# Routing the tokens once for groups of blocks instead of once for each block

## The chip, the cores and the metric

The kernel runs on one core of a Trainium2 chip. The metric is the device time of one execution in microseconds (us). TensorE (PE) does the matrix products, VectorE (DVE), ScalarE (ACT) and GpSimd (POOL) the element work, SyncE (SP) issues most of the transfers. PEld is TensorE's loading of weights.

## The reference

Three layers follow one another on 8 batches of 576 tokens, 4608 tokens of 512 values. First a landmark attention with 8 heads of 64, for each batch:

```
q_lm, k_lm = means of 18 consecutive rows of q and of k           # 32 landmarks
A, Bm, C   = softmax(q k_lm'), softmax(q_lm k_lm'), softmax(q_lm k)
Z          = Bm' / (norms of Bm);  6 times: Z = 2 Z - Z Bm Z
x          = A Z C v
```

Then a mixture of 8 experts with one expert for each token, where the routing is computed from the attention's output, and at last a dense layer with a squared relu:

```
logits = x @ w_gate;  expert = argmax(logits)
gate   = exp(logits - max) / (sum + 1e-9), at the argmax           # = 1 / (sum + 1e-9)
y      = gate * (relu(x @ w1[expert]) @ w2[expert])
out    = relu(y @ w_in)^2 @ w_out
```

## The kernel before, in words

There are three stages: the attention (`phase_a`), the experts (`phase_m1`), the dense layer (`phase_m2`). The attention works on a block at a time; a block is one batch, and its 576 tokens lie as 96 partitions (`PR`) of 6 tokens each (`R`). A block passes through parts, each written as a generator whose steps end at a `yield`: `load*`, `front` (transposes of q and k, landmarks), `head` (the small matrix Bm), `mid` (C v), `newton` (the six iterations), `amap` (the map A), `xout` (logits, and the output rows sent to `x_rows` in HBM) and `rout` (the routing). Block 0's routing also turns the order of the experts (`ro["perm"]`, `ro["key"]`), from which `wpre` loads the first expert's weights ahead.

`xout` makes the logits on TensorE and DVE transposes them to `lg`, 96 partitions x 6 tokens x 32, of which 8 are used (line 592). `rout` (lines 612 to 687) takes from them, for each of a block's 6 columns of 96 tokens: the maximum, the one-hot choice `oh`, the sum of the exponentials, the gate `gt`, and the rank of each token among those of its expert. The rank counts the tokens of the same expert in earlier partitions (a triangle of ones), in earlier columns of the block (a matmul with ones for each column), and in the earlier blocks, whose counts are kept in `ro["cnt"]`; all of it is summed in one bank `pr` on TensorE (lines 652 to 656). The rank is split into a place within a tile of 128 tokens and the tile's base (`ro["a128"]`), and `ro["ohv"]` keeps for each column a matrix of the places, 96 x 128 (line 684, once for each column). A block's gate is sent to the last column of `x_rows` by a transfer of SP's queue (line 667). Line numbers are those of the kernel before.

Who reads the routing: `prer` runs once, behind the routing of block 5; from `oh`, `a128` and `ohv` of blocks 0 to 5 it makes the lists of tokens of the first three tiles (`gpre`, `spre`), and POOL gathers these rows from `x_rows` (line 84). `prea`, `preb` and `prec` work on those tiles (the experts' first products) while the last blocks' attention runs. `tiles` runs behind the routing of block 7 and makes the lists of all 46 tiles, and then the stage of the experts begins.

The order of the work is given by the table `WHEN`: for each part, and for some blocks of their own, the due times of its first and last step, in units of a block's period. The steps of all parts and blocks are sorted by due time and traced in that order; a part is traced only when those that it needs have been (`rout` needs `xout` of its block and the routing before it). The framework then lays out the queue of each engine from this order by estimated costs, and puts in the waits. Each engine works its queue in order. Of the tiles of the routing there are two buffers each (pool `as`).

Of the kernel before, what the change touches and what calls it, by code (L numbers as in the profile page):

```python
# [7 lines left out]
F32 = mybir.dt.float32  # L8
F16 = mybir.dt.float16
I32 = mybir.dt.int32  # L10
U32 = mybir.dt.uint32
AF = mybir.ActivationFunctionType
ALU = mybir.AluOpType
# [4 lines left out]
B, H, S, D = 8, 8, 576, 64  # L18
NE, DM, FF = 8, 512, 1024
DF = 2048  # L20
NT = B * S
PR, R = 96, 6
LM = 32
XW = DM + 1
# [6 lines left out]
NBIG = 6  # L31
GB = 3
NG = -(-B // GB)
LMS = (0, 0)
RHE = ("VPPA", "PPPP")
EVE, EVA, QP = 2, 0, 1
# [207 lines left out]
def phase_a(tc, cst, q, k, v, wg, x_rows, x2, ro, rt, w12, wb, held):  # L244
    nc = tc.nc
    V, P, ACT, PE = nc.vector, nc.gpsimd, nc.scalar, nc.tensor
    with (
# [12 lines left out]
        for i in range(2):  # L260
            t = a1.tile([128, 2, 4, 64], F32, name=f"bd{i}")
# [14 lines left out]
        def small():  # L276

            turns[0] ^= 192
            return nb[:, turns[0]:turns[0] + 192]
# [6 lines left out]
        def big(name):  # L286
            return psb.tile([128, 512], F32, tag="b", name=name)

        st = [dict() for _ in range(B)]

        def load(nm, src):
            def one(b):
# [10 lines left out]
        for i in range(2):  # L303
            t = a1.tile([128, 2, 256], F32, name=f"wbd{i}")
            P.memset(t, 0.0)
            wbds.append(t)
            t = a1.tile([128, 32], F32, name=f"nrm{i}")
            P.memset(t, 0.0)
            nrm.append(t)
            t = a1.tile([128, 2, 32], F32, name=f"G{i}")  # L310
# [3 lines left out]
        def front(b):  # L314
# [5 lines left out]
            for ti, nm in enumerate(("q", "k")):  # L320
# [3 lines left out]
                for hf in range(2):  # L324
# [10 lines left out]
                    yield  # L335
                m = 4 if LMS[ti] == 2 else 5
                for g in range(-(-24 // m)):
                    n = min(m, 24 - m * g)
                    pt = big("pt")
                    for i in range(n):  # L340
                        j, r = divmod(m * g + i, R)
                        PE.transpose(pt[:, PR * i:PR * i + PR], rhs[j // 2][:, r, 128 * (j % 2):128 * (j % 2) + 128],
                                     ident[:PR, :PR])
                    if LMS[ti] == 2 and g % 3 == 2:

# [235 lines left out]
        def xout(b):  # L581
            s = st[b]
            AT, wbd, G = s["AT"], s["wbd"], s["G"]

            pl = small()
            for qd in range(2):
                av = AT[:, qd].rearrange("p (r a) -> p r a", r=R)
                for g in range(3):
                    PE.matmul(pl[32 * g:32 * g + 32, 0:192], G[:, qd, :], av[:, :, 32 * g:32 * g + 32],
                              start=(qd == 0), stop=(qd == 1))  # L590
            s["lg"] = lg = asm.tile([PR, R, 32], F32, tag="lg", name="lg")
            V.transpose(lg.rearrange("p r e -> p (r e)"), pl[:PR, 0:192])
            yield
            rows = x_rows[b * S:(b + 1) * S, :].rearrange("(p r) c -> p r c", r=R)
            t0 = 0
            for n in (128, 128, 128, 96, 96):
                px = big("px")
                for qd in range(2):
                    PE.matmul(px[:n, 256 * qd:256 * qd + 256], AT[:, qd, t0:t0 + n], wbd[:, qd, :],
                              start=True, stop=True)  # L600
                xr = a1.tile([128, DM], F32, tag="xr", name="xr", bufs=3)
                ACT.activation(xr[:n], px[:n], AF.Copy)
                i = 0
                while i < n:
                    r, p0 = divmod(t0 + i, PR)
                    m = min(n - i, PR - p0)
                    nc.sync.dma_start(out=rows[p0:p0 + m, r, 0:DM], in_=xr[i:i + m])
                    i += m
                t0 += n
                yield  # L610

        def rout(b):

            s = st[b]
            lg = s["lg"][:, :, 0:NE]
            bc = slice(b * R, (b + 1) * R)

            def over(t):
                return t.rearrange("p (r o) -> p r o", o=1).to_broadcast([PR, R, NE])
            mx = asm.tile([PR, R], F32, tag="mxl", name="mxl")  # L620
            V.tensor_reduce(out=mx, in_=lg, axis=AX.X, op=ALU.max)
            yield
            eq = asm.tile([PR, R, NE], F32, tag="eq", name="eq")
            V.tensor_tensor(eq, lg, over(mx), op=ALU.is_equal)
            V.tensor_tensor(lg, lg, over(mx), op=ALU.subtract)
            yield

            V.tensor_tensor(eq, eq, ro["ev"].rearrange("p (o e) -> p o e", o=1).to_broadcast([PR, R, NE]), op=ALU.mult)
            ACT.activation(lg, lg, AF.Exp)
            yield  # L630
            m = asm.tile([PR, R], F32, tag="m", name="m")
            V.tensor_reduce(out=m, in_=eq, axis=AX.X, op=ALU.max)
            yield
            key = ro["key"]
            if b == 0:

                pm = small()
                PE.matmul(pm[:, 0:1], sel, m[:, 0:1], start=True, stop=True)
                V.tensor_scalar(ro["m0"], pm[:, 0:1], -1.0, None, op0=ALU.mult)
                V.tensor_scalar(ro["perm"], ro["e8"], ro["m0"][:, 0:1], None, op0=ALU.add)  # L640
                V.tensor_scalar(ro["perm"], ro["perm"], 7, None, op0=ALU.bitwise_and)
                V.tensor_scalar(key, ro["perm"], -1.0, 8.0, op0=ALU.mult, op1=ALU.add)
            oh = ro["oh"][:, bc]
            V.tensor_tensor(oh, key[:PR].rearrange("p (o e) -> p o e", o=1).to_broadcast([PR, R, NE]), over(m),
                            op=ALU.is_equal)
            se = asm.tile([PR, R], F32, tag="se", name="se")
            V.tensor_reduce(out=se, in_=lg, axis=AX.X, op=ALU.add)
            yield

            pr = big("pr")  # L650
            prv = pr[:PR, 0:R * NE].rearrange("p (r e) -> p r e", e=NE)
            PE.matmul(prv, ro["tri"], oh, start=True, stop=False)
            for r in range(R - 1):
                PE.matmul(prv[:, r + 1:], ro["ones"][:, 0:PR],
                          oh[:, r:r + 1].to_broadcast([PR, R - 1 - r, NE]), start=False, stop=False)
            PE.matmul(prv, ro["ones"][:, 0:PR],
                      ro["cnt"].rearrange("p (o e) -> p o e", o=1).to_broadcast([PR, R, NE]), start=False, stop=True)
            cr = asm.tile([PR, NE], F32, tag="cr", name="cr")
            V.tensor_reduce(out=cr, in_=oh.rearrange("p r e -> p e r"), axis=AX.X, op=ALU.add)
            V.tensor_scalar(se, se, 1e-9, None, op0=ALU.add)  # L660
            yield
            rk8 = asm.tile([PR, R, NE], F32, tag="rk8", name="rk8")
            V.tensor_tensor(rk8, prv, oh, op=ALU.mult)
            V.tensor_tensor(ro["cnt"], ro["cnt"], cr, op=ALU.add)
            gt = asm.tile([PR, R], F32, tag="gt", name="gt")
            V.reciprocal(gt, se)
            nc.sync.dma_start(out=x_rows[b * S:(b + 1) * S, DM:XW].rearrange("(p r) c -> p (r c)", r=R), in_=gt)
            yield
            rk = asm.tile([PR, R], F32, tag="rk", name="rk")
            V.tensor_reduce(out=rk, in_=rk8, axis=AX.X, op=ALU.add)  # L670
            yield
            ri = asm.tile([PR, R], I32, tag="ri", name="ri")
            V.tensor_copy(ri, rk)
            yield
            V.tensor_scalar(ri, ri, 127, None, op0=ALU.bitwise_and)
            yield
            bf = asm.tile([PR, R], F32, tag="bf", name="bf")
            V.tensor_copy(bf, ri)
            yield
            V.tensor_tensor(ro["a128"][:, bc], rk, bf, op=ALU.subtract)  # L680

            for r in range(R):
                c = b * R + r
                V.tensor_scalar(ro["ohv"][:, c], ro["ib"], bf[:, r:r + 1], ro["tv"][:, c:c + 1],
                                op0=ALU.is_equal, op1=ALU.mult)
                if r == 2:
                    yield
            yield

# [101 lines left out]
        def tiles(b):  # L791
# [39 lines left out]
            for h in range(NH):  # L831
# [13 lines left out]
                yield  # L845
            mk = T2([128, NG, NTL])
            piv = pi[:, 0:NG * NTL].rearrange("p (g t) -> p g t", g=NG)
            V.scalar_tensor_tensor(mk, piv, 0.0, ro["gof"], op0=ALU.is_gt, op1=ALU.mult)
# [103 lines left out]
        ev = []  # L952
# [9 lines left out]
def consts_r(nc, pool):  # L962
# [6 lines left out]
    def iota(t, pattern, base=0, mult=0):  # L969
# [633 lines left out]
```

## Time and profile before

| what | value |
| --- | --- |
| runs | 1357.51, 1361.43 and 1367.07 us, median 1361.43 |
| profiled execution | 1361.7 us |
| its span | 1360.0 us |
| its mean granted clock of TensorE | 0.985 of full speed |
| instructions | 41279 |
| PE busy | 1307.0 us, 96% of the span |
| DVE busy | 999.0 us, 73% |
| ACT busy | 737.3 us, 54% |
| POOL busy | 570.3 us, 42% |

The profile is of one execution. The busy time of an engine is the time in which it worked on some instruction; matmuls are pipelined and their ends are modelled, so a busy PE need not be PE at its peak. The attention stage is the first 283 us or so of the span, the experts run until about 680 us, the dense layer to the end.

### The profile page before, as it was taken

How to read it: one execution, taken by the hardware profiler on the slowest of the kernel's cores; microseconds unless marked ns; L12 is line 12 of the kernel's file. 1: busy time of each engine (PE TensorE's matmuls, PEld its weight loads, DVE VectorE, ACT ScalarE, POOL GpSimd, SP SyncE). 2: the span in 40 equal slices, each digit the busy share in tenths (PEclk: the TensorE clock that was granted, in tenths of full speed). 3: DMA queues.
4: the chain of work that ended last, by engine and by line, in shares of the span. 5: the costliest groups of instructions: out<-in, count | busy, mean ns of one | idle time of the engine just before them, and what ended most of it. 6: DMA issues, size and time to landing. Idle time of an engine off the chain costs nothing. (4 is left out here: it accounts for less than half of the span.)

```text
span 1360.0 us, 41279 instructions
## 1 busy us (share of the span) xinstructions
PE 1307.0 (96%) x16614; PEld 1074.3 (79%) x16614; DVE 999.0 (73%) x2655; ACT 737.3 (54%) x1388; POOL 570.3 (42%) x584
## 2 busy tenths in 40 slices
PE   6889889899999999999999999999999999999997
PEld 4556556567777777777688999999999999999996
DVE  6788998866768668875399767777777777767665
ACT  4445556444657456754356555555555555555554
POOL 4435554223434335564300344444444444454443
PEclk9788999999999999999999999999999999999999
DMA  9676965355577648465110111111111110111100
GB/s 209 134 183 155 208 154 136 95 198 137 172 197 239 144 116 238 122 147 105 59 32 25 24 33 33 33 21 29 33 33 33 33 31 19 33 33 33 33 2 32
DMA packets 131535, 126.68 MB, mean 93 GB/s; under 512 B 88704, under 2 KB 107136, under 8 KB 131328
## 3 DMA queue, kind: packets, MB, share of 16 engines
q1 hardware_dynamic: 121568, 93.92, 29.9%
q0 software_dynamic: 9120, 29.95, 6.8%
q8 instruction: 133, 2.18, 0.7%
q14 instruction: 74, 0.61, 0.2%
q10 hardware_dynamic: 640, 0.02, 0.0%
HBM read 215.03 MB, written 28.89 MB: 179 GB/s over the span
## 5 line engine op out<-in xcount | busy, mean ns | idle before, releaser
L1415 POOL TENSOR_TENSOR hq<-q,hq 128x896 f16<-128x896 f32 x127 | 239.8, 1888 | 308.4 <-ACT hq L1410 235.1
L1423 PE MATMUL o<-wo,hq 128*128 128x256 f16 x3024 | 355.7, 273 | 1.2 <-DVE hq L1415 0.7
L1423 PEld LDWEIGHTS <-hq 128*128 128x128 f16 x3024 | 290.0, 98 | 35.8 <-DVE hq L1415 1.0
L1389 DVE TENSOR_TENSOR q<-h,q 128x256 f32<-128x256 f32 x508 | 186.7, 388 | 135.4 <-ACT q L1398 110.2
L1403 ACT ACTIVATE q<-q 128x512 f32<-128x512 f32 x127 | 80.1, 630 | 220.1 <-DVE q L1389 220.1
L139 PE MATMUL py<-wb,hT 128*128 128x512 f16 x864 | 192.4, 379 | 0.1
L124 PE MATMUL ph<-xT,wb 128*128 128x128 f16 x1120 | 189.5, 219 | 1.9 <-ACTq L1042 1.9
L126 PE MATMUL ph<-xT,wb 128*128 128x128 f16 x1120 | 189.4, 219 | 0.5 <-DVEq L1042 0.5
L125 PE MATMUL ph<-xT,wb 128*128 128x128 f16 x1120 | 189.5, 219 | 0.0
L139 PEld LDWEIGHTS <-hT 128*128 128x128 f16 x864 | 83.0, 98 | 94.0 <-issue 0.4
L1410 ACT ACTIVATE hq<-q 128x896 f16<-128x896 f32 x144 | 136.0, 944 | 27.1 <-DVE q L1343 25.6
L1383 PE MATMUL h<-sx,wb 128*128 128x128 f16 x762 | 134.3, 219 | 0.8 <-DVE q L1389 0.8
L1384 PE MATMUL h<-sx,wb 128*128 128x128 f16 x762 | 134.3, 219 | 0.0
L1385 PE MATMUL h<-sx,wb 128*128 128x128 f16 x762 | 134.3, 219 | 0.0
L124 PEld LDWEIGHTS <-wb 128*128 128x128 f16 x1216 | 118.9, 98 | 6.3 <-ACTq L1042 2.2
L125 PEld LDWEIGHTS <-wb 128*128 128x128 f16 x1216 | 118.9, 98 | 4.6 <-issue 0.5
L126 PEld LDWEIGHTS <-wb 128*128 128x128 f16 x1216 | 118.9, 98 | 0.6 <-DVEq L1042 0.6
L130 DVE SCALAR_TENSOR_TENSOR hT<-ph,hT 128x512 f16<-128x512 f32 x72 | 49.6, 689 | 86.2 <-ACT hT L129 63.8
L129 ACT ACTIVATE hT<-ph 128x512 f16<-128x512 f32 x72 | 42.9, 595 | 123.5 <-PE ph L126 120.8
L1384 PEld LDWEIGHTS <-wb 128*128 128x128 f16 x1016 | 99.4, 98 | 0.9 <-issue 0.9
L1385 PEld LDWEIGHTS <-wb 128*128 128x128 f16 x1016 | 99.4, 98 | 0.0
L1383 PEld LDWEIGHTS <-wb 128*128 128x128 f16 x1016 | 99.3, 98 | 0.0
(349 smaller groups left out, 3169.2 us busy)
## 6 DMA issues: line engine op xcount, KB each, us to landing
stg<-in_moe_w SPq DMA_DIRECT2D x74, 2048.0 KB
qn<-in_q SPq DMA_DIRECT2D x16, 576.0 KB
kn<-in_k SPq DMA_DIRECT2D x16, 576.0 KB
vn<-in_v SPq DMA_DIRECT2D x16, 576.0 KB
fw<-in_moe_w_in SPq DMA_DIRECT2D x16, 512.0 KB
fw<-in_moe_w_out SPq DMA_DIRECT2D x16, 512.0 KB
x_rows<-xr SPq DMA_DIRECT2D x32, 192.0 KB
stg<-in_moe_w SPq DMA_DIRECT2D x16, 256.0 KB
```

The source lines that it names most:

```text
L124: nc.tensor.matmul(ph[:, f4], wh[:, c, fs], xT[:, c], start=(c == 0), stop=False)
L125: nc.tensor.matmul(ph[:, f4], wh[:, c, fs], xT[:, 4 + c], start=False, stop=False)
L126: nc.tensor.matmul(ph[:, f4], wl[:, c, fs], xT[:, c], start=False, stop=(c == 3))
L139: self.nc.tensor.matmul(py, hT[:, a, f], w[:, f], start=(i == 0), stop=(i == len(ps) - 1))
L1383: PE.matmul(ph[:, k], w(0, c), x(0, c), start=(c == 0), stop=False)
L1384: PE.matmul(ph[:, k], w(0, c), x(1, c), start=False, stop=False)
L1385: PE.matmul(ph[:, k], w(1, c), x(0, c), start=False, stop=(c == 1))
L1389: V.tensor_tensor(to, x, y, op=ALU.add)
L1403: ACT.activation(q[:, 3:7], q[:, 3:7], AF.Relu, scale=2.0 ** -8)
L1410: ACT.activation(hq[:, 0], s["q"], AF.Copy)
L1415: e.tensor_tensor(hq[:, 1], q, hq[:, 0], op=ALU.subtract)
L1423: PE.matmul(sums[k][:, z], hq[:, u, a], wo[:, x, f, w], start=(f == 0 and i == 0 and z == 0), stop=(f == 7 and i == 2), skip_group_check=True)
```

## The change

The routing is done for a group of blocks at a time, by the table `RG`: block 0; 1 and 2; 3, 4 and 5; 6; 7. The logits of a group's blocks are laid side by side in one tile `lg`. `rout` of a block that is not the last of its group returns at once; that of the last block runs the same instructions as before over `U` columns, 6 for each block of the group, in place of 6. The sums over earlier columns go over all columns of the group (line 654), so that the count of the earlier blocks is added once for each group. `ohv` is still made by one instruction for each column, and the gates are still sent by one transfer for each block, now one behind another. The due times in `WHEN` are unchanged.

```diff
+RG = ((0,), (1, 2), (3, 4, 5), (6,), (7,))
...
+        lgs, RM = {}, R * max(map(len, RG))
...
-            s["lg"] = lg = asm.tile([PR, R, 32], F32, tag="lg", name="lg")
+            grp = next(g for g in RG if b in g)
+            if b == grp[0]:
+                lgs[b] = asm.tile([PR, RM, 32], F32, tag="lg", name="lg")
+            o = R * (b - grp[0])
+            lg = lgs[grp[0]][:, o:o + R]
             V.transpose(lg.rearrange("p r e -> p (r e)"), pl[:PR, 0:192])
...
         def rout(b):
-            s = st[b]
-            lg = s["lg"][:, :, 0:NE]
-            bc = slice(b * R, (b + 1) * R)
+            grp = next(g for g in RG if b in g)
+            if b != grp[-1]:
+                return
+            b0, U = grp[0], R * len(grp)
+            lg = lgs[b0][:, 0:U, 0:NE]
+            bc = slice(b0 * R, b0 * R + U)
+
+            def wide(tag, last=(), dt=F32):
+                return asm.tile([PR, RM, *last], dt, tag=tag, name=tag)[:, 0:U]
...
-            mx = asm.tile([PR, R], F32, tag="mxl", name="mxl")
+            mx = wide("mxl")
             V.tensor_reduce(out=mx, in_=lg, axis=AX.X, op=ALU.max)
...
-            for r in range(R - 1):
+            for r in range(U - 1):
                 PE.matmul(prv[:, r + 1:], ro["ones"][:, 0:PR],
-                          oh[:, r:r + 1].to_broadcast([PR, R - 1 - r, NE]), start=False, stop=False)
+                          oh[:, r:r + 1].to_broadcast([PR, U - 1 - r, NE]), start=False, stop=False)
...
-            nc.sync.dma_start(out=x_rows[b * S:(b + 1) * S, DM:XW].rearrange("(p r) c -> p (r c)", r=R), in_=gt)
+            for i, c in enumerate(grp):
+                nc.sync.dma_start(out=x_rows[c * S:(c + 1) * S, DM:XW].rearrange("(p r) c -> p (r c)", r=R),
+                                  in_=gt[:, R * i:R * i + R])
...
-            for r in range(R):
-                c = b * R + r
+            for r in range(U):
+                c = b0 * R + r
                 V.tensor_scalar(ro["ohv"][:, c], ro["ib"], bf[:, r:r + 1], ro["tv"][:, c:c + 1],
                                 op0=ALU.is_equal, op1=ALU.mult)
-                if r == 2:
+                if r % 6 == 2:
                     yield
```

The other tiles of the routing (`eq`, `m`, `se`, `rk8`, `gt`, `rk`, `ri`, `bf`) are widened as `mx` is.

## Rows read from the trace of the kernel before

**Rows 1.** The page's part 1: busy us, share of the span, instructions.

```profile
PE 1307.0 (96%) x16614; PEld 1074.3 (79%) x16614; DVE 999.0 (73%) x2655; ACT 737.3 (54%) x1388; POOL 570.3 (42%) x584
```

**Rows 2.** Busy time by stretches of the span; the first line names the columns.

```profile
core 0: us, PE busy (x) PEld busy (x) DVE busy (x) ACT busy (x) POOL busy (x), PEclk, DMA share, GB/s
60.00:130.00 70.00, 65.19 (x927) 40.49 (x916) 58.93 (x190) 38.27 (x98) 30.32 (x26) 0.90 0.74 172
130.00:226.00 96.00, 84.17 (x1235) 53.60 (x1236) 89.96 (x275) 55.45 (x144) 53.21 (x50) 0.96 0.72 166
226.00:247.00 21.00, 20.16 (x361) 11.51 (x359) 18.20 (x84) 9.98 (x32) 4.62 (x4) 1.00 0.28 81
...
262.00:283.00 21.00, 20.12 (x301) 16.45 (x300) 20.86 (x104) 8.00 (x15) 0.32 (x1) 1.00 0.23 58
...
310.00:670.00 360.00, 359.87 (x4076) 262.09 (x4074) 253.00 (x463) 200.98 (x359) 161.47 (x266) 1.00 0.61 155
```

**Rows 3.** DVE's groups to 300 us: xcount | busy us, mean ns | idle before.

```profile
L574 DVE RECIPROCAL ar<-asum 128x18 f32<-128x18 f32 x16 | 4.1, 255 | 0.1
...
L664 DVE TENSOR_TENSOR cnt<-cnt,cr 96x8 f16<-96x8 f16 x8 | 3.7, 457 | 0.0
L673 DVE CAST ri<-rk 96x6 int32<-96x6 f32 x8 | 3.5, 440 | 0.0
...
L663 DVE TENSOR_TENSOR rk<-pr,oh 96x48 f32<-96x48 f32 x8 | 1.6, 196 | 0.0
...
L666 DVE RECIPROCAL gt<-se 96x6 f32<-96x6 f32 x8 | 1.4, 181 | 0.0
L670 DVE TENSOR_REDUCE rk<-rk 96x6 f32<-96x48 f32 x8 | 1.4, 176 | 0.0
...
L827 DVE TENSOR_TENSOR z<-oh,z 96x96 f32<-96x96 f16 x4 | 0.7, 245 | 0.0
```

**Rows 4.** Order in time on DVE: start us, us; block 3's cast, then block 7.

```profile
155.59 1.73 DVE L673 CAST ri<-rk 96x6 int32<-96x6 f32 x1
...
264.60 0.23 DVE L659 TENSOR_REDUCE cr<-oh 96x8 f32<-96x48 f16 x1
...
265.06 0.20 DVE L663 TENSOR_TENSOR rk<-pr,oh 96x48 f32<-96x48 f32 x1
```

**Rows 5.** Order in time on POOL, at that cast and at the first gather.

```profile
155.24 1.47 POOL L333 TENSOR_SCALAR rh<-qn 96x1536 f32<-96x1536 f32 x1 [1.54 <-issue]
156.68 0.61 POOL L701 TENSOR_SCALAR stg<-stg 128x512 f32<-128x512 f32 x1
...
252.58 1.20 POOL L84 DMA_INDIRECT z<-x_rows,gpre  x1 [0.72 <-DMA x_rows<-xr]
```

**Rows 6.** Order in time on DVE, block 5's logits to the gather's landing.

```profile
225.62 0.37 DVE L592 STREAM_TRANSPOSE lg<-nb 96x192 f32<-96x192 f32 x1
...
236.94 0.18 DVE L621 TENSOR_REDUCE mxl<-lg 96x6 f32<-96x48 f32 x1
...
244.85 1.10 DVE L684 TENSOR_SCALAR ohv<-ib,bf,tv 96x128 f16<-96x128 f32 x4
...
252.38 0.16 DVE L745 TENSOR_TENSOR spre<-z,pts 128x3 int32<-128x3 f32 x1
...
258.58 0.69 DVE L58 TENSOR_REDUCE zvn<-z 128x1 f32<-128x512 f32 x1 [2.70 <-DMA z<-x_rows,gpre]
```

**Rows 7.** Order in time on PE: block 5's rank sums, and the wait behind the gather.

```profile
240.94 0.37 PE L654 MATMUL pr<-oh,ones 96*96 96x40 f16 x5
...
260.01 0.53 PE L589 MATMUL nb<-AT,G 128*32 128x192 f32 x6 [2.56 <-DVE zvn L59]
```

**Rows 8.** ACT's groups to 300 us, columns as in rows 3.

```profile
L629 ACT ACTIVATE lg<-lg 96x48 f32<-96x48 f32 x8 | 1.9, 242 | 1.0 <-DVE lg L625 0.9
```

**Rows 9.** Order in time on SP's queue at block 5's gate.

```profile
243.37 0.60 SPq L667 DMA_DIRECT2D x_rows<-gt  x1
```

More of the change, by code (lines that the diff above doesn't have):

```diff
@@ L612, in rout @@
         def rout(b):
-            s = st[b]
-            lg = s["lg"][:, :, 0:NE]
-            bc = slice(b * R, (b + 1) * R)
+            grp = next(g for g in RG if b in g)
[6 more added lines that the diff above has]
+                return asm.tile([PR, RM, *last], dt, tag=tag, name=tag)[:, 0:U]
             def over(t):
-                return t.rearrange("p (r o) -> p r o", o=1).to_broadcast([PR, R, NE])
-            mx = asm.tile([PR, R], F32, tag="mxl", name="mxl")
+                return t.rearrange("p (r o) -> p r o", o=1).to_broadcast([PR, U, NE])
+            mx = wide("mxl")
             V.tensor_reduce(out=mx, in_=lg, axis=AX.X, op=ALU.max)
             yield
-            eq = asm.tile([PR, R, NE], F32, tag="eq", name="eq")
+            eq = wide("eq", (NE,))
             V.tensor_tensor(eq, lg, over(mx), op=ALU.is_equal)
@@ L626, in rout @@
             yield
-            V.tensor_tensor(eq, eq, ro["ev"].rearrange("p (o e) -> p o e", o=1).to_broadcast([PR, R, NE]), op=ALU.mult)
+            V.tensor_tensor(eq, eq, ro["ev"].rearrange("p (o e) -> p o e", o=1).to_broadcast([PR, U, NE]), op=ALU.mult)
             ACT.activation(lg, lg, AF.Exp)
             yield
-            m = asm.tile([PR, R], F32, tag="m", name="m")
+            m = wide("m")
             V.tensor_reduce(out=m, in_=eq, axis=AX.X, op=ALU.max)
@@ L643, in rout @@
             oh = ro["oh"][:, bc]
-            V.tensor_tensor(oh, key[:PR].rearrange("p (o e) -> p o e", o=1).to_broadcast([PR, R, NE]), over(m),
+            V.tensor_tensor(oh, key[:PR].rearrange("p (o e) -> p o e", o=1).to_broadcast([PR, U, NE]), over(m),
                             op=ALU.is_equal)
-            se = asm.tile([PR, R], F32, tag="se", name="se")
+            se = wide("se")
             V.tensor_reduce(out=se, in_=lg, axis=AX.X, op=ALU.add)
@@ L650, in rout @@
             pr = big("pr")
-            prv = pr[:PR, 0:R * NE].rearrange("p (r e) -> p r e", e=NE)
+            prv = pr[:PR, 0:U * NE].rearrange("p (r e) -> p r e", e=NE)
             PE.matmul(prv, ro["tri"], oh, start=True, stop=False)
-            for r in range(R - 1):
+            for r in range(U - 1):
                 PE.matmul(prv[:, r + 1:], ro["ones"][:, 0:PR],
-                          oh[:, r:r + 1].to_broadcast([PR, R - 1 - r, NE]), start=False, stop=False)
+                          oh[:, r:r + 1].to_broadcast([PR, U - 1 - r, NE]), start=False, stop=False)
             PE.matmul(prv, ro["ones"][:, 0:PR],
-                      ro["cnt"].rearrange("p (o e) -> p o e", o=1).to_broadcast([PR, R, NE]), start=False, stop=True)
+                      ro["cnt"].rearrange("p (o e) -> p o e", o=1).to_broadcast([PR, U, NE]), start=False, stop=True)
             cr = asm.tile([PR, NE], F32, tag="cr", name="cr")
@@ L661, in rout @@
             yield
-            rk8 = asm.tile([PR, R, NE], F32, tag="rk8", name="rk8")
+            rk8 = wide("rk8", (NE,))
             V.tensor_tensor(rk8, prv, oh, op=ALU.mult)
             V.tensor_tensor(ro["cnt"], ro["cnt"], cr, op=ALU.add)
-            gt = asm.tile([PR, R], F32, tag="gt", name="gt")
+            gt = wide("gt")
             V.reciprocal(gt, se)
-            nc.sync.dma_start(out=x_rows[b * S:(b + 1) * S, DM:XW].rearrange("(p r) c -> p (r c)", r=R), in_=gt)
+            for i, c in enumerate(grp):
+                nc.sync.dma_start(out=x_rows[c * S:(c + 1) * S, DM:XW].rearrange("(p r) c -> p (r c)", r=R),
+                                  in_=gt[:, R * i:R * i + R])
             yield
-            rk = asm.tile([PR, R], F32, tag="rk", name="rk")
+            rk = wide("rk")
             V.tensor_reduce(out=rk, in_=rk8, axis=AX.X, op=ALU.add)
             yield
-            ri = asm.tile([PR, R], I32, tag="ri", name="ri")
+            ri = wide("ri", dt=I32)
             V.tensor_copy(ri, rk)
@@ L676, in rout @@
             yield
-            bf = asm.tile([PR, R], F32, tag="bf", name="bf")
+            bf = wide("bf")
             V.tensor_copy(bf, ri)
```

## Prediction

> **What bounds the kernel now.** I read the busy line of the page first, then the table by stages, then the groups of DVE instructions, and last the order in time around block 5. The page [rows 1] gives PE 96% of the span; but the change lies in the attention stage, which ends near 283 us, and PE's share there is another one. By stages [rows 2] PE is busy 359.87 of 360 us from 310 to 670 us: nothing after the attention stage waits for anything but PE, so whatever the attention stage gains or loses goes to the end of the kernel, and nothing else can. Inside it two engines are nearly full: from 130 to 226 us DVE has 90.0 of 96 us and PE 84.2 of 96. DVE is the fuller one, and every instruction of the routing but the sums over tokens, one exponential and one transfer per block is DVE's.
>
> The last part matters most. The routing of block 5 feeds the tiles worked ahead: its last `ohv` ends near 245.9, the scatter indices come at 252.38 [rows 6], POOL issues the first gather of token rows at 252.58 [rows 5], and DVE stands idle 2.70 us until they land at 258.58 [rows 6]; PE idles 2.56 us behind that [rows 7]. From 262 to 283 DVE is busy 20.86 of 21 us [rows 2]. So the end of the stage hangs on that gather: whatever moves it moves the end, nearly one to one.
>
> **What the change removes from DVE.** A block's routing has 17 short DVE instructions beside the six `ohv`. Eight sets become five, so 51 instructions go. Their price: the 17 groups of the view sum to 34.8 us for eight blocks, the costliest being the count update (457 ns mean), the cheapest the rank sum (176) [rows 3]; that is 4.35 us a block, the upper bound. Neighbours overlap, though: five such instructions in a row start within 0.46 us, 0.115 us apart [rows 4], so a packed set holds the queue for only 17 x 0.115 = 1.95 us, the lower bound. I take the means less an overlap of 0.08 us each: 4.35 - 1.36 = 3.0 us, nearer to the means because in the blocks concerned DVE and POOL are both loaded. Three sets: 9.0 us (5.9 to 13.0).
>
> The means are well above the packed price because some of these small instructions take over a microsecond: the cast `ri` has a mean of 440 ns [rows 3], and one of them took 1.73 us from 155.59 [rows 4] while POOL ran two instructions from 155.24 to 157.29 [rows 5]. It ended as POOL's second did. The Trainium skill ("SBUF — State Buffer", section "Who interferes with whom") says that casts, copies, scalar operations in a two-port mode and two-input operations of VectorE wait for a whole GpSimd instruction on a shared port pair, and the reverse. That row agrees; by that rule the wait belongs to the moment, and the next such DVE instruction would inherit it, so that the removed sets would be worth the lower bound and the gain worked out below would shrink from 3.2 to about 1.3 us.
>
> **What it makes longer.** Ten of the 17 run over 8 values per token. From 96x48 to 96x96 such an instruction goes from 196 to 245 ns [rows 3], 0.05 us per block added: the group of two costs 10 x 0.05 = 0.5 us more, the group of three 1.0. The other seven go from 6 to 12 or 18 values; a reciprocal takes 181 ns at 6 and 255 at 18 [rows 3], so at most 0.8 us in all, and most are cheaper: I take 0.1. Together 1.6 us (1.5 to 2.3). Net on DVE: 9.0 - 1.6 = 7.4 us less (3.6 to 11.5).
>
> **What it moves.** The 48 `ohv` stay, but six move from block 1 to block 2, and twelve from blocks 3 and 4 to block 5. Four of them took 1.10 us in block 5 [rows 6], 0.27 each: 3.3 us. So before block 5's routing DVE has (3.0 - 0.5) + 2 x 3.0 + 3.3 = 11.8 us less to do, and in it 1.0 + 0.1 + 3.3 = 4.4 us more, ahead of the gather.
>
> **PE.** A set of U columns takes U + 1 matmuls: 56 before, 21 + 13 + 19 = 53 after. Five of them took 0.37 us in block 5 [rows 7], 0.074 each, and the group of three has 12 more: 0.9 us. These are up to 136 columns wide where that row has up to 40, so 3.4 times as much, 3.0 us, is the upper bound, and nothing (they overlap with the work behind them) the lower; I take 0.9, by the row of the same chain. For PE as a whole it is nothing, but in block 5 these 0.9 us stand between `oh` and the ranks.
>
> **ACT, SP, transfers.** Three exponentials of 0.24 us go [rows 8] and two become wider; ACT is busy 55 of 96 us [rows 2] and nothing queues on it here, so nothing; without that cover, under a microsecond either way. Still eight gate transfers, but those of blocks 3, 4 and 5 stand behind one another on SP, 0.60 us each [rows 9]: the rows of block 5 queued behind them would go out 1.2 us later. SP was at 243.37 there, 9 us ahead of the gather; I take nothing (0 to 1.2). The transfers of blocks 1, 3 and 4 go later, but nobody reads them before the gather. POOL has no instruction of the routing; its gathers stand in its queue ahead of the last normalisation of block 7, which waits with them. The logits of a group stay in their buffer for up to three blocks; there are two buffers, and the one that the next group needs has been free since the group before last, so no wait arises there.
>
> **The sum.** Freed DVE time becomes earlier time only where DVE sets the pace. Of the idle time from 130 to 226 us 11.8 is PE's and 6.0 DVE's: PE waits for the others about two thirds of the time that somebody waits. I take 0.6 (0.15 to 0.9): 11.8 x 0.6 = 7.1 us earlier at block 5's routing. There 4.4 + 0.9 = 5.3 us are added on the way to the gather; DVE's idle time from 226 to 247 is 2.8 us [rows 2], in scraps, and I let half of it swallow 1.4: 3.9 remain. The gather, and the end of the stage, come 7.1 - 3.9 = 3.2 us earlier. The profiled execution took 1361.7 us (its span of 1360.0 and 1.7 around it), which is 0.3 above the median of the runs shown: 1361.7 - 3.2 = **1358.5 us**.
>
> **Rivals.** *No change.* PE is the real pace and DVE only looks full: a share of 0.3 frees 3.5 us, and block 5 takes 3.9: 1362.1. For it speaks PE's 65.2 of 70 us from 60 to 130; against it, that DVE is the fuller engine after 130. Chance 0.22.
>
> *Slower by block 5.* The three blocks' `ohv` and wider chain stand directly ahead of the gather and nothing hides them: 5.3 us, plus 1.2 on SP, is 6.5 us; if the freed time converts at only 0.15 (1.8 us), the stage ends 4.7 us later: 1366.4. It decides below a share of 5.3 / 11.8 = 0.45. For it speaks that DVE already waits 2.70 us for that gather and is full afterwards; against it, that block 5's routing started at 236.94, long after its logits at 225.62 [rows 6], so a DVE with less behind it can start it sooner. Chance 0.22.
>
> *More than forecast.* The share is 0.9 and the queues are laid out so that block 5's routing fills what was freed: 10.6 us less some 1.6 that stay on the way, 9 us, 1352.7. For it speaks the 94% of DVE; against it, PE's 84 of 96 us, which leaves at most 11.8 us there. Chance 0.13.
>
> That the change does less than it says is not likely: the first group is block 0 alone, so the expert's weights that wait for block 0's routing are not delayed, and the returns of the other blocks issue nothing.
>
> **How the numbers follow.** Forecast (1 to 7 us faster) 0.43, the three rivals 0.22, 0.22 and 0.13. The queues of this stage are laid out anew from estimated costs whenever an instruction goes, which can shift a few microseconds either way in every case; the range takes that in: 1350 to 1367. The forecast's own range is 1354.5 to 1360.5. A measurement of this kernel tells some 1% (13.6 us) from no change: faster than that needs more than the 11.8 us freed ahead of block 5 (0.04), slower needs more than twice the priced chain (0.04), within it 0.92.
>
> **What would show it.** Right: 85 short routing instructions on DVE instead of 136; DVE's time up to 262 us lower by 4 to 11 us; the first gather issued 2 to 5 us before 252.58, with DVE's idle time ahead of the landing no shorter than 2.7; the stage from the first gather on as long as before. Wrong: the gather at 252.58 or later (block 5 decided), or DVE with the same total (the waits on POOL were inherited), or PE idle as before with DVE idle grown by what was freed (PE set the pace).

## The result, and the profile after

The changed kernel took 1375.2 us (median of six executions, 1372.06 to 1383.93), the kernel before 1361.89 beside it (six, 1357.51 to 1367.07). The ratio is 1.0085 [1.0059, 1.0111], so 11.6 us slower (0.0085 x 1361.89; the two medians themselves lie 13.3 us apart); forecast were 1358.5 and a range up to 1367. The profiled execution happens to be the slowest of the six, 1383.93 us with a span of 1382.2; the other five end at 1379.11 or below. Read the rows for where the time went; the size of the loss is the ratio's.

Line numbers have moved: the logits' transpose is L598 now, the routing L633 to L698, the Newton steps L493, L508 and L514. The page's part 1 of the changed kernel (busy us, share of the span, instructions):

```profile
PE 1321.1 (96%) x16611; PEld 1085.3 (79%) x16611; DVE 989.8 (72%) x2604; ACT 737.3 (53%) x1385; POOL 571.9 (41%) x584
```

Against [rows 1] DVE has exactly the 51 instructions less that the change takes out, and 9.2 us less work. PE has three matmuls less and is 14.1 us longer at them. The stretches of [rows 2] in the changed kernel, same columns:

```profile
core 0: us, PE busy (x) PEld busy (x) DVE busy (x) ACT busy (x) POOL busy (x), PEclk, DMA share, GB/s
60.00:130.00 70.00, 64.07 (x948) 41.19 (x948) 56.68 (x172) 37.58 (x97) 29.32 (x24) 0.89 0.64 154
130.00:226.00 96.00, 83.75 (x1185) 53.85 (x1185) 74.82 (x224) 53.31 (x138) 51.87 (x49) 0.89 0.71 173
226.00:247.00 21.00, 19.60 (x211) 11.28 (x209) 17.08 (x65) 11.10 (x33) 6.35 (x6) 0.83 0.38 96
247.00:262.00 15.00, 13.61 (x201) 8.90 (x202) 4.41 (x15) 3.01 (x8) 1.16 (x1) 0.51 0.07 3
262.00:283.00 21.00, 14.43 (x190) 8.71 (x187) 15.45 (x66) 4.90 (x13) 6.71 (x6) 0.84 0.33 94
...
310.00:670.00 360.00, 357.52 (x4087) 261.72 (x4085) 254.71 (x468) 204.31 (x365) 160.95 (x258) 1.00 0.64 170
```

From 226 us on the granted clock is 0.83, 0.51 and 0.84, where [rows 2] have 1.00 from 226 to 247 and from 262 to 283; the stretch between these two was, before:

```profile
247.00:262.00 15.00, 11.52 (x174) 7.62 (x174) 10.91 (x48) 5.88 (x14) 6.59 (x6) 1.00 0.44 117
```

From 247 to 262 PE is now busy 13.61 of 15 us and DVE 4.41, with 10.91 before: PE works at the lower of its levels and DVE has nothing to do. To compare the whole stage, take it from the first block's logits to the first gather of the expert stage; that is one row for each kernel, before and after:

```profile
67.44:282.68 215.24, 193.39 (x2840) 124.30 (x2837) 191.40 (x683) 112.72 (x290) 89.77 (x82) 0.95 0.62 148
```

```profile
69.80:305.99 236.19, 206.96 (x2842) 134.51 (x2839) 181.85 (x633) 112.94 (x288) 89.49 (x82) 0.86 0.56 134
```

The stage is 20.95 us longer with 9.55 us less on DVE. What the clock withheld is the length times what is missing from 1.0: 215.24 x 0.05 = 10.8 us before, 236.19 x 0.14 = 33.1 after. That is 22.3 us more, as much as the lengthening; it is an upper bound for the clock's part, because not all of the stage waits on PE. By PE's own columns 13.57 us of the lengthening are busy time and 7.38 us are idle time (206.96 and 29.23 against 193.39 and 21.85). How the lower level looks in the rows, and what it makes DVE wait for (order in time on the changed kernel; the bracket gives the idle time before and what ended it; "remote" and "issue" name no engine):

```profile
240.09 0.53 PE L508 MATMUL nb<-u 32*32 32x96 f32 x16
248.59 1.72 PE L485 MATMUL pv<-vn,eT 96*32 96x64 f32 x54
250.23 1.22 PE L557 MATMUL pa<-qT,bd 128*64 128x288 f32 x2
252.84 0.86 PE L508 MATMUL nb<-u 32*32 32x96 f32 x16 [1.39 <-DVE u L493]
...
248.74 0.17 DVE L544 COPY G<-nb 128x16 f32<-128x16 f32 x1 [2.33 <-PE nb L541]
252.50 0.29 DVE L493 TENSOR_TENSOR u<-pv,rs 128x128 f32<-128x128 f32 x1 [3.58 <-remote]
254.89 0.48 DVE L559 STREAM_TRANSPOSE A<-pa 128x288 f32<-128x288 f32 x1 [2.11 <-PE pa L557]
...
264.10 0.38 DVE L598 STREAM_TRANSPOSE lg<-nb 96x192 f32<-96x192 f32 x1 [0.33 <-PE nb L591]
...
274.93 1.20 POOL L85 DMA_INDIRECT z<-x_rows,gpre  x1 [1.55 <-DVE spre L759]
```

Sixteen matmuls of the same form take 0.53 us at 240 and 0.86 at 253. Block 6's logits come at 264.10, 31.04 us behind block 5's at 233.06; before it was 20.94 (225.62 to 246.56). The first gather goes out at 274.93, against 252.58 in [rows 5].

### The profile page after: what moved, and what is told of

Same layout as the page of the kernel before. It is cut to its first block, busy times and chain, and to the rows that moved or that the text cites. A ratio compares the mean times of both kernels' runs of the same rounds, so it can differ in the third digit from the quotient of the medians.

```text
span 1382.2 us, 41209 instructions
## 1 busy us (share of the span) xinstructions
PE 1321.1 (96%) x16611; PEld 1085.3 (79%) x16611; DVE 989.8 (72%) x2604; ACT 737.3 (53%) x1385; POOL 571.9 (41%) x584
## 4 chain that ended last, share of the span: by engine, by line
PE 45%; DMA 3%; issue 1%; DVE 1%; ACT 1%; SPq 0%; POOL 0%; POOLq 0%; ACTq 0%; DVEq 0%
PE o L1437 22%; PE h L1397 7%; PE h L1398 7%; PE h L1399 7%; DMA x<-xr,sidx 3%; PE h L1367 1%; PE h L1365 1%; PE h L1366 1%; DVE q L1403 1%; DMA fa<-x 0%; ACT hq L1424 0%; ACT q L1417 0%; DVE out L1403 0%; SPq L1288 0%; DVE rr L1403 0%
## 5 line engine op out<-in xcount | busy, mean ns | idle before, releaser
L1424 ACT ACTIVATE hq<-q 128x896 f16<-128x896 f32 x144 | 136.0, 945 | 26.2 <-DVE q L1357 22.2
```

The lines of the kernel that those rows point to most:

```text
L1424: ACT.activation(hq[:, 0], s["q"], AF.Copy)
```

## Experiments

The theories in the expectations. **A**: block 5's longer chain ahead of the gather costs the time, my own rival. **B**: the planner lays the queues anew, and in the new order PE waits in other places and its clock falls. **C**: the grouping itself costs, by its lumps or by routing later. **F**: where the fetch of PE's instructions falls decides which waits are long. **L** and **P** come up last. Every ratio is to the kernel before, run beside it, and is the one on record; the quotient of the two medians can lie up to 0.003 from it (e5's is 1.0091).

### Which group does it

Only the list of groups differs from the changed kernel:

```
e1_pair        RG = ((0,), (1, 2), (3,), (4,), (5,), (6,), (7,))
e2_triple      RG = ((0,), (1,), (2,), (3, 4, 5), (6,), (7,))
e3_five_alone  RG = ((0,), (1, 2), (3, 4), (5,), (6,), (7,))
```

> The change with only blocks 1 and 2 grouped (0; 1 and 2; 3; 4; 5; 6; 7). Theory A (the loss is block 5's longer chain ahead of the gather and of PE's list matmuls): block 5 is as before, so 1358 to 1362 us, ratio 0.997 to 1.000, granted clock about 0.985. Theory B (any instruction removed lays the queues out anew, PE waits in new places, and the granted clock falls): slower by 4 to 10 us, 1366 to 1372, clock 0.976 to 0.981, with low-clock stretches between 140 and 230 us that the kernel before does not have.

> The change with only blocks 3, 4 and 5 grouped. Theory A: the whole loss or nearly, 1371 to 1376 us, with the first gather at 268 us or later and the clock at half speed somewhere from 240 to 262 us. Theory B: slower by 4 to 10 us as the pair alone, and not more than it.

> Blocks 1 and 2, and 3 and 4 grouped, block 5 by itself: 34 short DVE instructions fewer, and nothing added ahead of the gather. Theory A: 1355 to 1362 us, clock 0.983 or more. Theory B: slower, 1366 to 1376 us, clock 0.980 or less.

Measured: 1373.81 us, 1.0072 [1.0053, 1.0091]; 1369.64, 1.0045 [1.0021, 1.0069]; 1369.44, 1.0023 [1.0005, 1.0040]. The group of 1 and 2 alone loses nearly all, and it leaves block 5 as it was. That speaks against A. The parts don't add up either: all groups together lose 1.0085, not 1.0072 and 1.0045 on top of each other.

### Block 5's chain alone

In the kernel before, twelve further `ohv` in block 5's routing, ahead of the gather, whose result nobody reads:

```
+            if b == PB - 1:
+                for i in range(12):
+                    V.tensor_scalar(ro["ohx"][:, i], ro["ib"], bf[:, i % R:i % R + 1], ro["tv"][:, i:i + 1], ...
```

> The kernel before, with 12 more instructions like `ohv` in block 5's routing, into a tile that nobody reads: only what the change adds ahead of the gather, nothing removed, and the queues up to block 5 stay nearly as they were (18 lines of PE's queue differ). Priced at 12 x 0.27 = 3.3 us. Theory A: 3 to 12 us slower, first gather at 256 us or later, PE idle before its list matmuls. Theory B: within 2 us of the price or below it, 1361 to 1365.

Measured: 1365.2 us, 1.0011 [0.9988, 1.0035]. The gather does go out later, as the row on POOL shows:

```profile
256.14 1.20 POOL L84 DMA_INDIRECT z<-x_rows,gpre  x1 [1.61 <-DVE lg L625]
```

3.56 us later than in [rows 5], and yet the program's end moves by 1.5 us; its interval holds none at all, and at most 4.8 us (0.0035 of 1364). So A does not explain the loss of 11.6: a later gather was not what decided.

### A new order without any change of the work

In the kernel before only due times are moved; no instruction is added or taken out. e5 moves the attention map of blocks 2 to 5 by 0.02 of a block, e6 the routing of blocks 1 to 4 by 0.1:

```
e5  -amap=(0.42, 1.043)     +amap=(0.44, 1.063)
e6  -rout=(2.638, 2.696)    +rout=(2.738, 2.796)
```

> The kernel before with no instruction changed; only the due times of `amap` in blocks 2 to 5 are 0.02 of a block later, which lays the queues out anew about as far from the kernel before as the change does (74 and 196 lines of PE's and DVE's queue without the routing, the change 95 and 280). Theory B (it is the new layout that costs, whatever made it new): 4 to 10 us slower, 1367 to 1374 us, granted clock 0.982 or less. Theory C (the grouping itself costs: the routing in two lumps, DVE idle where PE is not ready): within 2 us of the kernel before, 1362 to 1366, clock 0.984.

> The kernel before with no instruction changed; the routing of blocks 1 to 4 is due 0.1 of a block later (64 and 198 lines differ). Theory B: 4 to 10 us slower. Theory C: within 2 us of the kernel before.

Measured: 1376.32 us, 1.0118 [1.0049, 1.0186], and 1382.4, 1.0149 [1.0098, 1.0200]. Moves of a due time alone lose as much as the change or more, and more than the 4 to 10 us that B had. The stretch from 130 to 226 us in e5 and in e6:

```profile
130.00:226.00 96.00, 78.20 (x1086) 48.66 (x1085) 79.20 (x241) 50.17 (x131) 49.65 (x47) 0.86 0.61 151
```

```profile
130.00:226.00 96.00, 82.83 (x969) 50.59 (x968) 76.45 (x244) 46.27 (x123) 44.89 (x41) 0.81 0.61 147
```

The clock is 0.86 and 0.81 where [rows 2] have 0.96, and DVE does 11 to 14 us less in the stretch than the 89.96 there, though it has the same work to do.

One try to tune the changed kernel's due times (routing of 1 and 2 later, of 3 to 5 earlier: `rout2=(2.9, 3.3)`, `rout5=(2.45, 2.507)`):

> The changed kernel with the routing of the group 1 and 2 due later and spread (2.9 to 3.3 in place of 2.638 to 2.696) and that of 3, 4 and 5 earlier (2.45 to 2.507): the same instructions in another layout. Theory B: another layout gives another time, anywhere from 1360 to 1376, with the clock following it. Theory C: 1372 to 1378, since the lumps are the same.

Measured: 1382.46 us, 1.0157 [1.0111, 1.0202]. Another order, another loss, and a larger one than either theory had.

### The place of PE's instructions

The same order, moved by 64 or 128 small matmuls at the start of the program, in the changed kernel (e7, e10) and in the kernel before (e9):

```
+        for _ in range(64):
+            PE.matmul(pv[:, 256:288], cst["identh"], cst["identh"][:, 0:32], start=True, stop=True)
```

> The changed kernel with 64 small matmuls at the very start, where PE waits for the first loads; the order of all else is the same on every engine. In the changed kernel's trace PE stands still inside a row of like matmuls (2.9 us at 154, 1.9 at 219) with nothing to wait for, until a block of its instructions has been fetched. Theory F (where the blocks of PE's instructions end decides those waits, and they start the low-clock stretches): the waits move, and the time changes by 3 us or more either way from the 1375 of the changed kernel. Theories B and C: 1372 to 1378 as the changed kernel.

> The kernel before with 64 small TensorE matmuls (32 columns) at the start of the program; the order on every engine is otherwise the same. 64 of them cost at most 2 us where nothing hides them. F (where the fetch of TensorE's next instructions falls decides which of its waits are long): the program is moved against the boundaries, so waits of 1 to 3 us move to other places; the time may move by up to 6 us to either side, as the grouped kernel's did (1375.2 to 1368.6), and the waits above 0.7 us between 60 and 310 us add up to another sum than 17.6. B alone (only the order decides): the same time as before, 1364, plus 0 to 2. If it is 1364 to 1366 with the same waits at the same lines, F is no part of the loss.

> The kernel after with 128 small TensorE matmuls at the start in place of 64; order otherwise the same as after. F: the boundaries lie elsewhere again, so the time differs from both 1375.2 (none) and 1368.6 (64 of them), and may lie anywhere from 1362 to 1380; the wait of 2.9 us inside the row of like matmuls at 154 us is not in that place. If instead it is the extra work at the start that lifts the granted clock (a warm-up), the time falls on: 1368 or below, with the granted clock in the first 100 us higher than with 64. If 64 gained by chance alone, 1375.

Measured: e7 1368.55 us, 1.0035 [1.0008, 1.0063]; e10 1371.52, 1.0039 [1.0023, 1.0055]; e9 1363.66, 0.9999 [0.9982, 1.0017]. The theory came from a wait in the changed kernel with nothing to wait for, within a row of 32 like matmuls:

```profile
153.74 0.53 PE L485 MATMUL pv<-vn,eT 96*32 96x64 f32 x21
157.18 0.64 PE L485 MATMUL pv<-vn,eT 96*32 96x64 f32 x11 [2.92 <-issue]
```

and what the transfers did from 153 to 158 us there (their busy tenths in 40 slices, then packets, MB and share by queue):

```profile
DMA  9999989999998774220001010100000000000000
...
q1 hardware_dynamic: 313, 0.50, 42.7%
q8 instruction: 1, 0.02, 1.6%
```

The data transfers fill the engines at first, but are nearly over at 155.3, and PE stands still until 157.18, so they do not account for the second half of the wait. The one transfer of the queue named "instruction" is a packet of 16 KB that starts at 154.50 and lands at 155.77, and PE goes on 1.4 us behind that. In the traces of all runs PE has sixteen such waits of more than 1 us from 60 to 310 us, in nine of the kernels: each time such a packet is under way, and PE goes on 1.1 to 1.5 us after it has landed. With 64 and with 128 matmuls more; e7, then e10:

```profile
149.69 0.42 PE L543 MATMUL nb<-wgt,WT 32*32 32x8 f32 x21 [2.27 <-issue]
```

```profile
155.81 0.41 PE L487 MATMUL pv<-vn,eT 96*32 96x64 f32 x11 [1.55 <-issue]
...
219.00 0.76 PE L487 MATMUL pv<-vn,eT 96*32 96x64 f32 x20 [2.45 <-issue]
```

Counted from the program's start, the first wait stands behind 1746 matmuls in the changed kernel and in e7 alike, so that in e7 it falls on a matmul that comes 64 earlier in the work. In e10 it stands behind 1874, which is 128 more and so the very matmul of the changed kernel, against what its expectation took for granted. So the place of the program decides where such waits fall; that is shown.

What it is worth is open. Both moved versions are six to seven us nearer to the kernel before than the changed kernel; their intervals end at 1.0063 and 1.0055 where its own begins at 1.0059. But e10 has its waits at the same matmuls as the changed kernel, and in the kernel before the move changes the waits (those over 0.7 us from 60 to 310 us add up to 23.7 us in place of 17.6) and not the time. Nor is it the clock: the mean over the executions is 0.977 in e7 and 0.976 in e10, as in the changed kernel (0.976), where before has 0.983 to 0.986. A warm-up by the added matmuls would have lifted that clock, and e10 has twice as many as e7 and is no faster. F is not shown to be a part of the loss, and what makes these two faster was not found.

### Late routing without grouping

In the kernel before, still eight sets, only due later (block 1's with block 2's, those of 3 and 4 with block 5's):

```
+            rout1=(3.58, 3.638), rout3=(4.484, 4.542), rout4=(3.542, 3.6),
...
-            s["lg"] = lg = asm.tile([PR, R, 32], F32, tag="lg", name="lg")
+            s["lg"] = lg = asm.tile([PR, R, 32], F32, tag="lg", name="lg", bufs=3)
```

> The kernel before, still eight sets of routing instructions, but block 1's routing is due with block 2's and those of blocks 3 and 4 with block 5's (their logits wait in a third buffer). Only the time of the routing moves; no instruction is saved and no set is wider. C (the lump of routing ahead of block 5 costs): DVE has about 6 us of blocks 3 and 4 routing ahead of block 5's gather: first gather past 258 us and 1366 to 1371. A new order (B): 1366 to 1380 with the granted clock lower and more of TensorE's waits, gather wherever it falls. If the grouping's saving was what cost something: 1364.

Measured: 1381.93 us, 1.0122 [1.0093, 1.0150], with the first gather at 276.38. That is above both ranges, just above B's and 11 us above C's. B is the nearer, but the late routing may be a part of it, here and in every result so far that contains a late group. What was missing was a kernel with the one and without the other.

### The grouping in the old order, the old routing in the new order

These four decide. Every instruction of the stage is noted as it is traced, and tied behind its predecessor in a written list; such a tie only orders the queue, it adds no wait between engines. The list is the order of the other kernel, without the routing, whose instructions find their places freely:

```
+PIN = dict(PE="...", DVE="...", Activation="...", Pool="...", SP="...")
...
+                for x in nc.cur_bb.bb.instructions[k0:]:
+                    made.setdefault((nm, b, str(x.engine).split(".")[-1]), []).append(x)
...
+        for eng, text in PIN.items():
+            last = None
+            for run in text.split():
+                nm, b, i, n = run.split(".")
+                for x in made[nm, int(b), eng][int(i):int(i) + int(n)]:
+                    if last is not None:
+                        tc.add_manual_dep(x, last.name, info, reason="pin")
+                    last = x
```

e12 is the changed kernel with the order of before on all engines, e13 the same with PE's list alone, e14 the kernel before with the order of after, e15 the kernel of e11 with the order of before.

> The kernel after (routing in groups), with every other instruction of the attention stage tied, engine by engine, to the order that it has in the kernel before; only the routing's own instructions find their places freely. B (the new order lost the time): the loss is gone, and what the grouping saves on DVE may show: 1356 to 1364, granted clock about as before's (0.984), first gather at 249 to 253 us. C (the grouping itself costs, by its lumps or its later routing): still 1370 to 1378. A (block 5's longer chain): 1367 to 1371 with the gather at 256 or later. My prediction's sum (3.2 us gained) would be 1361.

> The kernel after with TensorE's instructions alone tied to before's order; VectorE, ScalarE and the queues are left to the planner. If TensorE's order is what counts: 1358 to 1366, like e12_pin_all. If VectorE's order counts as much, its instructions now come at other times than TensorE wants them: 1368 to 1382.

> The kernel before (eight sets of routing), with every other instruction of the attention stage tied to the order that it has in the kernel after. B: this order loses the time whatever the routing: 1372 to 1382, first gather at 268 us or later, granted clock 0.98 or lower. C (grouping costs, not the order): 1362 to 1367. The DVE work that grouping saves comes on top: up to 7 us slower than after.

> The kernel of e11_moved (eight sets, the routing of block 1 due with block 2's and those of 3 and 4 with block 5's), with the other instructions tied to before's order. B: e11's 17 us of loss were its order: 1362 to 1368. C: the lump of late routing ahead of block 5's gather costs: about 6 us of DVE work (two blocks' 3.0 us) later, 1368 to 1372, gather at 256 to 259. If nothing of e11's loss goes away: 1380.

| | us | ratio |
|---|---|---|
| after | 1375.2 | 1.0085 [1.0059, 1.0111] |
| e14, routing of before, order of after | 1376.5 | 1.0086 [1.0060, 1.0112] |
| e12, routing of after, order of before | 1367.41 | 1.0006 [0.9988, 1.0024] |
| e13, the same, PE's order alone | 1367.67 | 1.0012 [0.9988, 1.0036] |
| e11, eight sets, due late | 1381.93 | 1.0122 [1.0093, 1.0150] |
| e15, the same in the order of before | 1368.09 | 1.0024 [1.0007, 1.0041] |

(Before, beside e12 to e15, took 1365.14.) The loss goes with the order and not with the grouping, in both directions: 1.0085 and 1.0086 with the one order, 1.0006 with the other. Tying PE's order alone is enough. (By the letter e12's 1367.41 us and its gather at 256.03 are what A expected; but before took 1365.14 beside it, and the ratio leaves A at most 0.0024, 3.3 us. e14's gather came at 264.20 and not at 268 or later.) How much the order costs is not one number: e7 and e10 have after's order too and lose 1.0035 and 1.0039. Late routing costs some 3 us (e15), and some 13 of e11's 17 were its order. The stretches in e12:

```profile
130.00:226.00 96.00, 85.31 (x1227) 54.87 (x1220) 80.70 (x235) 55.66 (x144) 52.14 (x49) 0.93 0.72 175
226.00:247.00 21.00, 17.40 (x335) 10.15 (x334) 18.84 (x80) 8.31 (x28) 3.48 (x3) 0.97 0.18 34
247.00:262.00 15.00, 12.59 (x167) 7.58 (x162) 9.71 (x41) 4.87 (x12) 6.60 (x6) 0.70 0.38 93
262.00:283.00 21.00, 20.11 (x262) 15.44 (x261) 19.92 (x104) 8.59 (x14) 0.00 (x0) 1.00 0.28 75
```

The clock is at 0.93 and 0.97 again where after had 0.89 and 0.83. But 0.9988 as the lower end also says that the grouping gains at most 1.6 us when nothing else changes, and e12's first gather is at 256.03, outside my 249 to 253.

### What the grouping gains in the old order

In e12, order in time on DVE and on PE around block 5's routing:

```profile
241.05 4.70 DVE L835 TENSOR_SCALAR ohv<-ib,bf,tv 96x128 f16<-96x128 f32 x18
245.67 0.14 DVE L872 TENSOR_SCALAR dv<-pc 128x1 f32<-128x1 f32 x1
245.85 0.15 DVE L873 TENSOR_TENSOR cnt<-cnt,dv 1x1 f16<-1x1 f16 x1
245.92 0.27 DVE L651 TENSOR_TENSOR u<-u,nb 128x128 f32<-128x128 f32 x1
...
242.67 0.70 PE L742 MATMUL px<-wbd,AT 128*128 128x256 f32 x2
246.25 1.50 PE L728 MATMUL nb<-AT,G 128*32 128x192 f32 x12 [2.87 <-DVE u L651]
```

All 18 `ohv` of the group stand in one row (L835), a Newton step (L651) of block 7 stands behind them, and PE has nothing for 2.87 us until that step has read its `nb`; what PE then starts, the logits of block 6, writes a tile of that name. Before, two `ohv` of block 5 stood ahead of that step and four behind it. Theory **L**: this row gives the gain back. Rival **P**: PE sets the pace, and what DVE saves is worth nothing. e16 is e3's grouping (block 5 alone) in the order of before; e17 is e12 with one more tie, which lets the Newton step go ahead of the ninth `ohv`:

```
+        for x in made["rout", 5, "DVE"][17 + 8:]:
+            tc.add_manual_dep(x, made["newton", 7, "DVE"][2].name, info, reason="spread")
```

> The kernel of e3_five_alone (groups 0; 1 and 2; 3 and 4; 5; 6; 7) with the other instructions of the stage tied to before's order. Theory L (the row of 18 value instructions ahead of a Newton step is what gives the gain back): without blocks 3 and 4 in block 5's row, the wait of 2.87 us goes, the stage is 2 to 5 us shorter than in e12_pin_all and the time 1360 to 1363. Rival P (TensorE sets the pace of the stage, what VectorE saves is worth nothing): 1364 to 1367, as e12_pin_all. e3 without the ties was 1369.

> The kernel of e12_pin_all with the row of 18 value instructions divided: the third Newton step of block 7 goes ahead of the ninth of them. L: TensorE's wait of 2.87 us behind that step falls to under 1.2 us (8 of 18 instead of 18 of 18 are ahead of it); the time falls by 1 to 2 us against e12_pin_all, 1362 to 1366. P: the wait shrinks but the time stays within 1 us of e12_pin_all.

Measured: e16 1362.15 us, 0.9994 [0.9975, 1.0013]; e17 1362.78, 1.0000 [0.9980, 1.0019] (before beside them 1362.68). PE's waits of over 0.7 us in e17 around the divided row:

```profile
244.78 0.53 PE L645 MATMUL nb<-u 32*32 32x96 f32 x16 [1.27 <-DVE asum L711]
246.39 0.66 PE L879 MATMUL pi<-z,ohv 96*128 96x3 f16 x20 [1.08 <-DVE z L870]
```

The logits of block 6 no longer wait, but 1.27 + 1.08 = 2.35 us stand again ahead of other matmuls, one of them the sums over the `ohv` themselves: what DVE makes behind that row was late all the same. In e16 the longest wait on PE from 200 us to the gather's landing is 0.82 us, as long as before's longest there (0.83). The ratios go the way of L (1.0006, 1.0000, 0.9994), but their intervals overlap, and e17's expected 1 to 2 us against e12 can't be told from nothing. So neither L nor P is shown. No version beat the kernel before by more than its interval.

## Why the prediction was wrong, point by point

**What bounds the kernel.** That the stage's gain or loss goes to the end of the program held: the stage is 20.95 us longer and the profiled execution 22.2 (1383.93 against 1361.7). That the end of the stage hangs on block 5's gather did not hold: e4 moved the gather by 3.56 us and the program by 1.5, with none inside its interval.

**DVE's saving** was right. 51 instructions went; 7.4 us were forecast (3.6 to 11.5), and the stage's rows give 191.40 - 181.85 = 9.55; in e12's profile, in the old order, the stage's 184.10 gives 7.30. The size of a wider instruction was right too; DVE's groups in the changed kernel, at 48, 96 and 144 elements:

```profile
L675 DVE TENSOR_TENSOR rk<-pr,oh 96x48 f32<-96x48 f32 x3 | 0.6, 203 | 0.1
...
L675 DVE TENSOR_TENSOR rk<-pr,oh 96x96 f32<-96x96 f32 x1 | 0.3, 254 | 0.9 <-PE pr L668 0.9
L675 DVE TENSOR_TENSOR rk<-pr,oh 96x144 f32<-96x144 f32 x1 | 0.3, 304 | 0.7 <-PE pr L668 0.7
```

0.05 us per block, as worked out. The price by which the waits on POOL would be inherited did not come true for the cast and the count update, whose means fell from 440 and 457 ns [rows 3] to below 280 and 160; one inherited wait is there, an `eq` of 1.10 us from 235.31 that ended 0.16 us behind a POOL instruction (235.09 to 236.25). That row agrees with the rule cited from the Trainium skill ("SBUF — State Buffer", section "Who interferes with whom"); the means say that few of the later instructions met such a moment. How many do goes with the order: the same 85 short instructions add up to 17.9 us in the changed kernel and to 23.1 in e12, where 136 of them took 34.8 before.

**The step that failed** is the sum's treatment of the order. It converts freed DVE time into earlier time by a share of 0.6 (0.15 to 0.9) within the order of the queues as it was, and puts the new order at nothing: the queues "are laid out anew ... which can shift a few microseconds either way", which only widened the range. The planner laid them anew, and that order costs 10.8 us (1.0085 - 1.0006 = 0.0079 of 1364), as e12 and e14 show, or 4.8 and 5.3 us where the program is moved (e7, e10). It was neither small nor symmetric: e5, e6, e8 and e11, other orders, give 16, 20, 21 and 17 us, none of them a gain. I had one order to judge by and no run of another. A rival with that mechanism, priced by the clock of the stretches (1.00 against 0.90 in [rows 2], so 2 us in 21), was missing.

**The share** itself was not shown wrong. With PE's order held, block 5's logits come 156.26, 148.80 and 150.96 us after the first logits in the profiles of e12, e13 and e17, against 158.18 before: 1.9, 9.4 and 7.2 us earlier, where I had 7.1. These are single profiles at different clocks, and the spread is as large as the size.

**Block 5's chain** was mis-sized. 5.3 us were added, 3.9 of them after what idle time swallows; in e12 the way from block 5's logits to the gather is 34.57 us (221.46 to 256.03) against 26.96 [rows 5, 6], 7.6 more, part of it at a clock of 0.70; in e13 and e17 it is 32.55 and 32.17, so 5.6 and 5.2 more. In the old order this takes back about what the share frees, and the time is that of the rival "No change", whose mechanism, PE as the pace, was not shown. But the chain did not decide the loss: e4's delay of the gather costs at most 0.0035 of 1364 = 4.8 us and by its ratio 1.5. The rival built on it was nearest in sign and wrong in cause, since e1, which leaves block 5 alone, loses 1.0072. Its sign, a gather at 252.58 or later, came true at 274.93 by the new order, so that sign could not tell the two apart.

**PE** was costed at 0.9 us for its wider rank sums. That PE's granted clock could fall stood nowhere in the sum; in the changed kernel's profile up to 33.1 us are withheld against 10.8. That the clock carries the whole loss is not shown, and two rows speak against it. e7 has an execution of 1364.82 us at the clock of 0.979 at which the changed kernel took 1372.06. And the stage of e14, in the same order, is 14.48 us longer than before's, of which 5.82 are PE's busy time, where a lower clock shows directly, and 8.66 its idle time:

```profile
64.95:294.67 229.72, 199.21 (x2845) 129.34 (x2842) 196.38 (x684) 113.37 (x291) 89.62 (x81) 0.91 0.57 138
```

**What is still open.** Why after's order lets the clock fall is read from rows only: PE's work stands bunched from 247 to 262 us while DVE waits for it. Which of its displaced instructions begins that was not found; no run changed the clock and nothing else. Why the same order loses less than half as much when the program is moved by 64 or 128 matmuls is open too.

## What to carry to other kernels

Where queues are laid by a planner from estimated costs, a change of a few instructions is two changes: the work, and a new order. In this stage the second was several times the first, and the pair of runs that told them apart was the new work tied to the old order and the old work tied to the new. Before forecasting, give the new order a rival of its own, with a price from rows: how much of the stage runs at the full clock and without waits in the present order, and what the stretches lose that do not.

## What the runs showed of the hardware

Of one and the same program the time falls as the granted clock rises, in two kernels nearly one to one. After's executions go from 1372.06 us at 0.979 to 1383.93 at 0.969, 11.9 us for 0.010 (0.010 of the span is 13.8); e12's from 1360.54 at 0.990 to 1370.98 at 0.980, 10.4 us. It is not the clock alone: e1 took 1368.03 and 1373.16 us at 0.983. From 310 to 1340 us the clock is 1.00 in the profiles of the changed kernel and of the one before, so nearly all that differs in it lies ahead of that.

PE can stand still within a row of like matmuls that wait for no engine, for 1.1 to 2.9 us. In all sixteen such waits over 1 us a 16 KB packet of the instruction queue was under way, and PE went on 1.1 to 1.5 us after it had landed. The places go with the count of matmuls from the program's start (1746 in the changed kernel and in e7, 1874 in e10), so 64 matmuls more move such a wait to another instruction of the work, and 128 more bring it back to the same one. Many packets land without a wait: the kernel before has no such wait over 1 us from 60 to 310 us.
